# Sparse attention and a two-layer projection on one core: the first three batches run as sequences of their own, w_out is loaded ahead of batch 2, and the masking and copying of these batches is spread over three engines

## The chip, the cores and the metric

The kernel runs on one core of one Trainium2 chip. The metric is the device time of one execution in microseconds (us); lower is better. Every timed kernel was run four times, and the kernel before was run beside it on the same chip. A profile is of one execution: its span is about 2 us shorter than the time of the same run, because the span is counted from the first to the last instruction. The granted clock, or PEclk, is the share of the full TensorE clock that the profile shows as granted, 1.00 at most.

Engine names are those of the profile: PE is TensorE, DVE is VectorE, ACT is ScalarE, POOL is GpSimd, SP is SyncE; a trailing q (SPq) is the queue from which that engine issues DMAs.

## The reference

```python
def _attn_ref(q, k, v):                      # each (8, 8, 576, 64): batch, heads, tokens, width
    B, H, S, D = q.shape
    stride = 32
    scores = np.matmul(q, k.transpose(0, 1, 3, 2)) / np.sqrt(D)
    rel = pos[:, None] - pos[None, :]
    mask_local = (rel >= 0) & (rel < stride)                      # heads 0 to 3
    mask_strided = (rel >= 0) & (pos[None] % stride == pos[:, None] % stride)   # heads 4 to 7
    ...                                      # masked softmax, then attn @ v

def _moe_ref(x, w_in, w_out, alpha):         # x: the 4608 tokens of attention output, 512 wide
    h = x @ w_in                             # 512 -> 2048
    g = np.maximum(h, 0.0) + alpha * np.minimum(h, 0.0)
    return g @ w_out                         # 2048 -> 512
```

So there are eight batches of attention, each with four local and four strided heads, and then two projections over 4608 tokens, which the kernel takes in nine chunks of 512.

## The kernel before

A batch has two units, the strided one and the local one. Each unit has two pairs of heads. The attention of a unit is cut into pieces: two transposes (T, of q and of k), three scores for each pair (Sc), two or three products with v for each pair (Pv), and one transpose of the output for each pair (X). The pieces that matter here:

```python
def transpose_piece(u, nm):
    tp = pspool.tile([128, 8, 64, 2], F16, tag="ps", name="tp")     # PSUM
    ...                                                             # 8 transposes on PE
    if nm == "q":
        for hh in range(2):                                         # two halves of 64 partitions
            rr = slice(64 * hh, 64 * hh + 64)
            keep(nc.vector.tensor_copy(split(qpads[u % 2][rr, :, hh, :])[0], main[rr]))
        return
    ...
    keep(nc.scalar.copy(ko[0], main))                               # kT
    keep(nc.scalar.copy(ko[1], tail(0, 128, 64)))
    ...

def score_piece(P, i):
    ...                                                             # matmuls into sp
    keep(nc.scalar.activation(et[0:r, 0:n], sp[0:r, 0:n], AF.Exp, scale=SCALE))
    eng = nc.vector if P.b < 2 else nc.gpsimd                       # who multiplies by the mask
    ...
        keep(eng.tensor_tensor(ev, ev, m..., op=ALU.mult))

def pv_piece(P, a):
    ...                                                             # matmuls into pv, et as weights
    keep(nc.vector.reciprocal(rc[0:w, 0:nb], pvv[:, :, 64]))
    keep(nc.vector.tensor_tensor(P.x16..., pvv[:, :, 0:64], rc..., op=ALU.mult))
```

The program order is written out by hand. Batch 0 is done before the first projection. From batch 1 on, one rolling sequence mixes the pieces of neighbouring pairs, and the pieces are dealt out between the matmuls of the projections; fp32 to fp16 casts of q, k and v go to GpSimd along with them.

```python
for m in range(16):
    lin1_piece(0, m, True)
    if m == 8:
        ...                                  # casts of batch 1's local unit, loads of batch 2
        for c in range(4):
            load_w(c, True)                  # w_out, issued by GpSimd between batch 2's loads
    attn_n(0 if m < 12 else 1, end1)
...
for n in range(1, NCH):                      # the main loop; one n is one round
    ab = attn_until(n + 2) if n + 2 < B else len(pieces)
    for i in range(16):
        lin2_piece(n, i)
        attn_step(ab)
        if n + 1 < NCH:
            lin1_piece(n + 1, i)
            attn_step(ab)
    while pos["i"] < ab:
        attn_step(ab)                        # what is left over, in a block
```

The softmax here doesn't subtract the row's maximum and nothing guards it: scores larger than these inputs give would overflow.

## Time and profile before

| | kernel before |
|---|---|
| time, median of its first 4 runs | 363.94 us (362.0 to 365.44) |
| span of the profile, granted clock | 363.0 us, 0.953 |
| busy: PE, DVE, ACT, POOL | 329.7, 226.5, 177.6, 138.7 us |
| first matmul of lin1(0), lin1(1), lin2(0) | 32.2, 79.3, 97.7 us |
| first matmul of the main loop, of its second round | 119.1, 153.7 us |
| from there to the end | 209.3 us |

The chain of waits leads back from the last instruction to whatever released it, step by step. Its shares tell which engine the end of the kernel waited for. In the kernel before it is PE for four fifths, and DMA for a tenth:

```profile
PE 81%; DMA 9%; DVE 3%; ACT 2%; POOL 2%; issue 2%; SPq 1%; POOLq 0%; ACTq 0%
```

An engine can be busy for 60% of the span, as DVE is, and hold the chain for 3% of it. The stage marks in the table are read from the timeline of PE.

### The profile page before, as it was taken

Reading aid. Unit: us, or ns where it says so; the run is one execution under the profiler, and the core shown is the slowest. Engines: PE = TensorE matmul, PEld = TensorE weight load, DVE = VectorE, ACT = ScalarE, POOL = GpSimd, SP = SyncE. Lnnn points to the kernel's source line nnn. Section 1 sums busy time; section 2 is a strip of 40 time slices with the busy share of each in tenths; the row PEclk is TensorE's granted clock in tenths of the full one; section 3 lists DMA queues with packets and bytes.
Section 4 is the critical chain, followed back from the end, with each engine's and each line's share of the span. In section 5 each row is a group of like instructions: output and inputs, shape, how many; then the busy total and the mean of one; then the engine's idle time right before and its main releaser. Section 6 shows DMA issues by size and latency. Waiting matters only on the chain.

```text
span 363.0 us, 6353 instructions
## 1 busy us (share of the span) xinstructions
PE 329.7 (91%) x2449; PEld 185.8 (51%) x2449; DVE 226.5 (62%) x423; ACT 177.6 (49%) x328; POOL 138.7 (38%) x170
## 2 busy tenths in 40 slices
PE   6658974649998999999999999999999999999996
PEld 3353443424564455555557776555555444444444
DVE  5776898837864477758676767585767444444410
ACT  2532663516643556565656565656554544444421
POOL 5360473381576365546455564556151000000000
PEclk9977997559999999999999999999999999999999
DMA  7989999999936083519352820000000010010012
GB/s 210 218 134 287 199 238 196 275 206 280 232 103 203 32 232 96 175 42 246 96 175 53 242 63 32 29 32 29 31 32 29 29 60 29 29 60 29 29 61 87
DMA packets 52926, 44.08 MB, mean 121 GB/s; under 512 B 33616, under 2 KB 38112, under 8 KB 52896
## 3 DMA queue, kind: packets, MB, share of 16 engines
q1 hardware_dynamic: 47712, 37.11, 38.8%
q0 software_dynamic: 4640, 5.51, 8.2%
q10 hardware_dynamic: 544, 1.05, 1.0%
q8 instruction: 19, 0.31, 0.4%
q14 instruction: 11, 0.09, 0.1%
HBM read 38.42 MB, written 9.44 MB: 132 GB/s over the span
## 4 chain that ended last, share of the span: by engine, by line
PE 81%; DMA 9%; DVE 3%; ACT 2%; POOL 2%; issue 2%; SPq 1%; POOLq 0%; ACTq 0%
PE hps L437 34%; PE ops L482 34%; DMA sttl<-in_k_dram 6%; PE sp L251 4%; PE tp L210 3%; PE pv L280 3%; DMA stv<-in_v_dram 3%; PE xp L297 2%; SPq L100 1%; PE ops L473 1%; DVE et L266 1%; DVE x L289 1%; ACT osb L487 1%; POOL vs L151 1%; ACT et L259 0%
## 5 line engine op out<-in xcount | busy, mean ns | idle before, releaser
L437 PE MATMUL hps<-xT,win 128*128 128x512 f16 (+1 forms) x640 | 148.3, 364 | 0.8 <-DVE gT L450 0.8
L450 DVE SCALAR_TENSOR_TENSOR gT<-neg,oma,hps 128x512 f16<-128x512 f32 x144 | 106.9, 743 | 59.2 <-ACT neg L447 56.7
L482 PE MATMUL ops<-wout,gT 128*128 128x512 f16 x560 | 141.4, 379 | 2.0 <-ACT osb L487 2.0
L447 ACT ACTIVATE neg<-hps 128x512 f32<-128x512 f32 x144 | 86.2, 599 | 94.9 <-PE hps L437 94.0
L266 POOL TENSOR_TENSOR et<-et,consts 128x384 f16<-128x384 f16 (+2 forms) x60 | 54.2, 908 | 85.4 <-ACT et L259 84.5
L437 PEld LDWEIGHTS <-win 128*128 128x128 f16 x640 | 60.1, 99 | 49.8 <-issue 6.0
L482 PEld LDWEIGHTS <-gT 128*128 128x128 f16 x560 | 50.4, 98 | 49.0 <-issue 2.8
L259 ACT ACTIVATE et<-sp 128x384 f16<-128x384 f32 (+2 forms) x96 | 45.6, 490 | 24.6 <-PE sp L251 24.4
L289 DVE TENSOR_TENSOR x<-pv,rc 72x384 f16<-72x384 f32 (+2 forms) x80 | 42.2, 527 | 2.7
L223 DVE COPY qpad<-tp 64x1024 f16<-64x1024 f16 x32 | 39.0, 1220 | 3.8 <-PE tp L210 3.5
L251 PE MATMUL sp<-qpad,kT 128*128 128x144 f16 (+1 forms) x224 | 32.8, 248 | 7.2 <-DVE qpad L240 3.8
L287 DVE RECIPROCAL rc<-pv 72x6 f32<-72x6 f32 (+2 forms) x80 | 14.8, 186 | 37.5 <-PE pv L280 37.3
L280 PEld LDWEIGHTS <-et 72*128 72x128 f16 (+1 forms) x448 | 25.6, 102 | 23.7 <-POOL et L262 3.7
L251 PEld LDWEIGHTS <-kT 128*128 128x128 f16 x224 | 20.5, 103 | 25.4 <-issue 5.7
L487 ACT COPY osb<-ops 128x512 f32<-128x512 f32 x35 | 20.5, 586 | 21.9 <-PE ops L482 21.9
L236 ACT COPY kT<-tp 128x1024 f16<-128x1024 f16 x16 | 16.2, 1011 | 20.0 <-PE tp L210 20.0
L280 PE MATMUL pv<-vl,et 128*128 128x65 f16 x192 | 12.4, 201 | 8.1 <-POOL et L262 3.4
L280 PE MATMUL pv<-vs,et 72*128 72x65 f16 x256 | 16.9, 200 | 1.7 <-DVE x L289 0.9
L151 POOL CAST vs<-stv 72x1024 f16<-72x1024 f32 x16 | 16.9, 1084 | 2.9 <-DMA stv<-in_v_dram 2.9
L297 PE MATMUL xp<-consts,x 72*128 72x72 f16 (+1 forms) x224 | 15.3, 211 | 2.0 <-DVE x L289 1.7
L297 PEld LDWEIGHTS <-x 72*128 72x128 f16 (+1 forms) x224 | 12.8, 104 | 7.2 <-DVE x L289 2.4
L151 POOL CAST tl<-sttl 128x512 f16<-128x512 f32 x8 | 4.9, 618 | 28.6 <-DMA sttl<-in_k_dram 28.6
(48 smaller groups left out, 186.4 us busy)
## 6 DMA issues: line engine op xcount, KB each, us to landing
out_dram<-osb SPq DMA_DIRECT2D x35, 256.0 KB, 2.0
stq<-in_q_dram SPq DMA_DIRECT2D x16, 512.0 KB, 6.7
stk<-in_k_dram SPq DMA_DIRECT2D x12, 512.0 KB, 5.0
stv<-in_v_dram SPq DMA_DIRECT2D x7, 768.0 KB
stv<-in_v_dram SPq DMA_DIRECT2D x8, 576.0 KB
win<-in_moe_w_in_dram POOLq DMA_DIRECT2D x4, 512.0 KB, 9.3
wout<-in_moe_w_out_dram POOLq DMA_DIRECT2D x4, 512.0 KB, 13.4
stk<-in_k_dram ACTq DMA_DIRECT2D x2, 512.0 KB, 8.4
```

Source lines behind the costliest of these rows:

```text
L151: keep(nc.gpsimd.tensor_copy(o, i))
L223: keep(nc.vector.tensor_copy(split(qpads[u % 2][rr, :, hh, :])[0], main[rr]))
L251: keep(nc.tensor.matmul(sp[:, 2 * w * x : 2 * w * x + 2 * w], P.kT[:, k0 : k0 + 128], P.qpad[:, :, w * t : w * t + w], start=(x == 0), sto ...
L259: keep(nc.scalar.activation(et[0:r, 0:n], sp[0:r, 0:n], AF.Exp, scale=SCALE))
L266: keep(eng.tensor_tensor(ev, ev, m.unsqueeze(1).to_broadcast([r, n // w, w]), op=ALU.mult))
L280: keep(nc.tensor.matmul(pv[:, 65 * x : 65 * x + 65], et[0:r, c : c + 128], v16[0:r, t, 2 * P.pr + hh, :], start=(x == 0), stop=(x == nb - ...
L289: keep(nc.vector.tensor_tensor(P.x16[0:w, c0 : c0 + 64 * nb].rearrange("r (c e) -> r c e", e=64), pvv[:, :, 0:64], rc[0:w, 0:nb].unsqueeze ...
L297: keep(nc.tensor.transpose(xp[:, P.w * t : P.w * t + P.w], P.x16[0 : P.w, 128 * t : 128 * t + 128], ident[0 : P.w, 0 : P.w]))
L437: keep(nc.tensor.matmul(hps[:, dst : dst + w], win16[:, kk, 128 * m : 128 * m + 128], xT[:, kk, src : src + w], start=(kk == 0 and x == 0) ...
L447: keep(nc.scalar.activation(neg, hps, AF.Relu, scale=-1.0))
L450: keep(nc.vector.scalar_tensor_tensor(gTs[n][:, m, :], neg, oma[:, m : m + 1], hps, op0=ALU.mult, op1=ALU.add))
L482: keep(nc.tensor.matmul(ops, gTs[n][:, kf, 128 * mt : 128 * mt + 128], wout16[:, kf, :], start=(kf == 0), stop=(kf == 15)))
```

## The change

The intent is to have the first three batches ready sooner. Each of them becomes a sequence of its own, in which both of its units are in flight, and no piece of a later batch stands ahead of its last pieces. w_out goes out before batch 2's loads rather than among them. For these batches, the mask multiplies alternate between DVE and GpSimd, and one of the two copies of a transposed q goes to ScalarE. Twelve buffers hold the exponentials (et) instead of eight. The first three steps of the main loop take no attention pieces, so that GpSimd gets ahead.

```diff
-    NE = 8
+    NE = 12
...
-                keep(nc.vector.tensor_copy(split(qpads[u % 2][rr, :, hh, :])[0], main[rr]))
+                copy = nc.scalar.copy if b < 3 and hh else nc.vector.tensor_copy
+                keep(copy(split(qpads[u % 2][rr, :, hh, :])[0], main[rr]))
...
-        eng = nc.vector if P.b < 2 else nc.gpsimd
+        eng = nc.vector if P.b < 3 and i % 2 == 0 else nc.gpsimd
...
+    def first(u0, u1, order):            # one batch: transposes, scores, pv, x of both units
+        ...
+    first(1, 0, 0)
+    first(2, 3, 1)
+    first(4, 5, 1)
...                                       # the rolling sequence starts with batch 3
...                                       # batch 0: w_in's quarters go out later (steps 8 and 15)
     for m in range(16):
         lin1_piece(0, m, True)
         if m == 8:
             ...
-            load_part(2, False, "qk")
-            ...
-            for c in range(4):
-                load_w(c, True)
         attn_n(0 if m < 12 else 1, end1)
+    cast_part(1, True, "q", 0, "pool")
+    cast_part(1, True, "k", 0, "pool")
+    for c in range(4):
+        load_w(c, True)
+    keep(nc.sync.dma_start(gate[:, 16:32], wout16[:, 7, 496:512]))
+    ...                                   # batch 2's loads, batch 1's strided v casts
     while pos["i"] < end1:
         attn_step(end1)
     for m in range(16):
         lin1_piece(1, m, True)
-        attn_n(0 if m < 8 else 1, end2)
+        attn_n(0, end2)
...                                       # casts of batch 2, loads of batch 3 among lin2(0)
+    cast_tail(3, "pool")                  # ahead of the main loop: casts of batch 3, loads of 4
+    cast_part(3, False, "q", 0, "pool")
+    ...
     for n in range(1, NCH):
         for i in range(16):
+            now = 0 if n == 1 and i < 3 else ab
             lin2_piece(n, i)
-            attn_step(ab)
+            attn_step(now)
```

More of the change, by code (lines that the diff above doesn't have):

```diff
@@ L324, in X, with sc, pv, tr @@
         return lambda: x_piece(pairs[g])
-    feed(T(1, "q"), 0)
-    feed(T(1, "k"), 0)
-    for g in (2, 3):
-        for i in range(3):
-            feed(Sc(g, i), 0)
-    for g in (2, 3):
-        for i in range(3):
-            feed(Pv(g, i), 0)
-    feed(T(0, "q"), 0)
-    feed(T(0, "k"), 0)
-    feed(X(2), 0)
-    feed(X(3), 0)
-    for g in (0, 1):
-        for i in range(3):
-            feed(Sc(g, i), 0)
-    for g in (0, 1):
-        for i in range(2):
-            feed(Pv(g, i), 0)
-    feed(X(0), 0)
-    feed(X(1), 3)
+    def first(u0, u1, order):
+        A, Bp = (2 * u0, 2 * u0 + 1), (2 * u1, 2 * u1 + 1)
+        def sc(gs):
+            for g in gs:
+                for i in range(3):
+                    feed(Sc(g, i), -1)
+        def pv(gs):
+            for g in gs:
+                for i in range(len(pairs[g].pgroups)):
+                    feed(Pv(g, i), -1)
+        def tr(u):
+            feed(T(u, "q"), -1)
+            feed(T(u, "k"), -1)
+        def xs(gs, last=False):
+            for g in gs:
+                feed(X(g), g if last else -1)
+        tr(u0)
+        sc(A)
+        if order == 0:
+            tr(u1)
+            sc(Bp)
+            pv(A)
+            xs(A)
+        else:
+            pv(A)
+            tr(u1)
+            xs(A)
+            sc(Bp)
+        pv(Bp)
+        xs(Bp)
+    first(1, 0, 0)
     end0 = len(pieces)
+    first(2, 3, 1)
+    end1 = len(pieces)
+    first(4, 5, 1)
+    end2 = len(pieces)
     casts = []
@@ L354, in plan_casts @@
         u = (g + 3) // 2
-        if u >= 2 * B or u < 2:
+        if u >= 2 * B or u < 7:
             return []
@@ L359, in plan_casts @@
         return [(b, strided, nm, pr) for nm, pr in names]
-    for g in range(3, npair + 2):
+    for g in range(11, npair + 2):
         a, p, t, x = g, g - 1, g + 1, g - 2
-        okA = 4 <= a < npair
-        okP = 4 <= p < npair
-        okT = 4 <= t < npair and t % 2 == 0
-        okX = 4 <= x < npair
+        okA = 12 <= a < npair
+        okP = 12 <= p < npair
+        okT = 12 <= t < npair and t % 2 == 0
+        okX = 12 <= x < npair
         nP = len(pairs[p].pgroups) if okP else 0
@@ L530 @@
     cast_tail(0, "pool")
-    cast_part(0, True, "v", 0, "pool")
-    cast_part(0, True, "v", 1, "pool")
-    cast_part(0, False, "v", 0, "pool")
-    load_w(0, False)
-    cast_part(0, False, "v", 1, "pool")
-    load_w(1, False)
-    load_w(2, False)
-    load_w(3, False)
     apt = pspool.tile([128, 512], F32, tag="ps", name="apt")
     for i in range(end0):
-        if i == 8:
-            cast_part(0, False, "q", 0, "dve")
-            cast_part(0, False, "k", 0, "act")
-        attn_step(end0)
-        if i < 2:
-            warm(4)
-        elif i < 14:
-            warm(1)
-        if i == 13:
+        if i == 2:
             keep(nc.vector.tensor_copy(id16, ident[0:16, 0:16]))
@@ L553 @@
                 oma, apt[:, 0:16], -1.0, 1.0, op0=ALU.mult, op1=ALU.add))
-    gate = cpool.tile([128, 16], F16)
-    keep(nc.sync.dma_start(gate, win16[:, 0, 1008:1024]))
+        if i == 5:
+            cast_part(0, True, "v", 0, "pool")
+        if i == 8:
+            cast_part(0, False, "q", 0, "dve")
+            cast_part(0, False, "k", 0, "act")
+            cast_part(0, True, "v", 1, "pool")
+            load_w(0, False)
+        attn_step(end0)
+        if i == 15:
+            cast_part(0, False, "v", 0, "pool")
+            load_w(1, False)
+            cast_part(0, False, "v", 1, "pool")
+            load_w(2, False)
+            load_w(3, False)
+        if i < 2:
+            warm(4)
+        elif i < 16:
+            warm(1)
+    gate = cpool.tile([128, 32], F16)
+    keep(nc.sync.dma_start(gate[:, 0:16], win16[:, 0, 1008:1024]))
     for strided in (False, True):
@@ L567, in attn_n @@
             attn_step(0)
-    end1 = attn_until(1)
     for m in range(16):
@@ L576 @@
             cast_part(1, False, "k", 0, "pool")
-            load_part(2, False, "qk")
             for pr in range(2):
                 cast_part(1, False, "v", pr, "pool")
-            load_part(2, False, "v")
-            for c in range(4):
-                load_w(c, True)
         attn_n(0 if m < 12 else 1, end1)
+    cast_part(1, True, "q", 0, "pool")
[3 more added lines that the diff above has]
+    keep(nc.sync.dma_start(gate[:, 16:32], wout16[:, 7, 496:512]))
+    load_part(2, False, "qk")
+    load_part(2, False, "v")
+    load_part(2, True, "qk")
+    for pr in range(2):
+        cast_part(1, True, "v", pr, "pool")
+    load_part(2, True, "v")
     while pos["i"] < end1:
         attn_step(end1)
-    end2 = attn_until(2)
     for m in range(16):
         lin1_piece(1, m, True)
-        attn_n(0 if m < 8 else 1, end2)
+        attn_n(0, end2)
+    cast_tail(2, "pool")
+    cast_part(2, False, "q", 0, "pool")
+    cast_part(2, False, "k", 0, "pool")
+    for pr in range(2):
+        cast_part(2, False, "v", pr, "pool")
+    load_part(3, False, "qk")
+    load_part(3, False, "v")
     for i in range(16):
@@ L592 @@
         attn_n(2, end2)
+        if i == 2:
+            cast_part(2, True, "q", 0, "pool")
+            cast_part(2, True, "k", 0, "pool")
+            load_part(3, True, "qk")
+        if i == 5:
+            for pr in range(2):
+                cast_part(2, True, "v", pr, "pool")
+            load_part(3, True, "v")
     while pos["i"] < end2:
         attn_step(end2)
+    cast_tail(3, "pool")
+    cast_part(3, False, "q", 0, "pool")
+    cast_part(3, False, "k", 0, "pool")
+    load_part(4, False, "qk")
+    for pr in range(2):
+        cast_part(3, False, "v", pr, "pool")
+    load_part(4, False, "v")
     for n in range(1, NCH):
@@ L598 @@
         for i in range(16):
+            now = 0 if n == 1 and i < 3 else ab
             lin2_piece(n, i)
-            attn_step(ab)
+            attn_step(now)
             if n + 1 < NCH:
                 lin1_piece(n + 1, i)
-                attn_step(ab)
+                attn_step(now)
         while pos["i"] < ab:
```

## The prediction

> **What bounds the kernel now.** I read the page first, part 2 above all, then the chain of waits cut to 20 to 125 us, then the timeline and the queue of DMA issues for the same stretch. Names: a batch has a local unit (heads 0 to 3) and a strided unit (4 to 7), each of two pairs of heads. lin1(n) and lin2(n) are the two projections of the n-th 512 tokens, 64 matmuls each. The main loop starts with lin2(1).
>
> ```profile
> PE   6658974649998999999999999999999999999996
> ...
> DVE  5776898837864477758676767585767444444410
> ...
> PEclk9977997559999999999999999999999999999999
> DMA  7989999999936083519352820000000010010012
> ```
>
> One digit is 9.07 us. From slice 13 (119 us) on, PE reads 8 or 9 to the end; before that it falls to 4 and its clock to half, while DMA reads 9. So the kernel has two regimes, and the change can win only in the first. The chain of waits for 20 to 125 us shows what sets that regime (start, duration, what):
>
> ```profile
> 32.20 10.46 PE hps L437 x40
> ...
> 44.42 13.93 DMA sttl<-in_k_dram
> ...
> 59.13 1.03 POOL q L151
> 60.16 1.14 POOL k L151
> 61.31 3.18 SPq L100
> 64.59 0.61 SPq L100
> 65.29 9.59 DMA stv<-in_v_dram
> 74.94 2.04 POOL vs L151 x2
> 76.97 0.88 POOL et L266
> ...
> 79.52 9.71 PE hps L437 x36
> ```
>
> lin1(0) starts at 32.2, lin1(1) only at 79.5. In between batch 1 should finish, but its last pieces stand behind pieces of batch 2 in PE's order, and those wait for batch 2's loads and GpSimd's casts. The timelines of GpSimd and of the DMA queue show why the loads are late:
>
> ```profile
> 45.03 2.99 POOL L493 DMA_DIRECT2D wout<-in_moe_w_out_dram  x4
> ```
>
> ```profile
> 44.42 0.78 SPq L109 DMA_DIRECT2D sttl<-in_k_dram  x1
> ...
> 46.37 18.11 SPq L100 DMA_DIRECT2D stq<-in_q_dram  x1
> ```
>
> w_out goes out in the middle of batch 2's loads; the tail then takes 13.9 us, and the next load is stuck in its issue for 18 us. Other marks from the same chain: lin2(0) starts at 97.7, the main loop at 119.1, its second round at 153.9.
>
> **What the Trainium skill says.** "Perfetto Trace Analysis", section "Optimizing Scalar/DVE Operations": work of a saturated DVE may go to ScalarE or GpSimd, but GpSimd and DVE share an SBUF read port, so moving work between those two may not help. The trace agrees: a 128x384 mask multiply on DVE had a mean of 0.38 us (L266), but the one at 50.0 us, beside GpSimd casts, took 1.21. "GPSIMD Engine Reference", 4.1: about 2 times slower for two inputs. It agrees (by shape, means in ns):
>
> ```profile
> L266 POOL TENSOR_TENSOR et<-et,consts 72x432 f16<-72x432 f16 x24 | 23.9, 998 | 18.3 <-ACT et L259 17.5
> ...
> L266 DVE TENSOR_TENSOR et<-et,consts 72x432 f16<-72x432 f16 x8 | 4.2, 539 | 1.8 <-ACT et L259 1.8
> ```
>
> "DMA: Bandwidth & Descriptors", "Issuing engines are not separate DMA queues": all queues interleave on the same 16 engines. It agrees: the 13.9 us tail beside w_out, against a least of 4.9. "TensorE: Matmul & The Clock Gate", "What's actually happening": half clock after an idle window of about 3.4 us, full again after as long a busy one. It agrees: PEclk is 0.5 from 60 to 80 us, and lin1(1)'s first 38 matmuls took 9.9 us against 38 x 0.2155 = 8.2, a cost of 1.7.
>
> **Batch 0: about -0.8 us.** Before, DVE is nearly full from 16.8 to 32.6 us. The change gives ScalarE one of two qpad copies in each of two transposes (2 x 1.22 us) and GpSimd 4 of 12 multiplies (about 1.8 us), so some 4 us leave DVE. But the scores of the second unit now stand ahead of the first unit's output in DVE's order. By hand: local cast ends 16.5, qpad 18.5, the tails after ScalarE's kT 20.1, scores 20.2, six exponentials of 0.5 to 23.5, multiplies 23.9; then six reciprocal and scale steps of 0.66 (27.9), four of 0.69 (30.7), xT. lin1(0) starts at 31.4 instead of 32.2.
>
> **w_in goes out later: against the change.** GpSimd's order now puts two local multiplies and a value cast before w_in's second quarter, which went out at 20.1 and now can at about 24.7. The gate for batch 1's loads reads that quarter. Before it opened at 28.6, with the first quarter in the way; I take 31.5, and batch 1's tail at 43.5 to 44 instead of 40.95. Its transpose stood at 45.1, so most of this fits in slack; I charge 0.5 to 1 us.
>
> **Batch 1 alone: the gain.** lin1(0) ends near 50.5 with two scores done. GpSimd ends the multiply of local score 2 at 52.4. Next in its order stand the strided q and k casts (2.1), the issue of w_out (3.0) and two value casts (2.1), and only then the multiply of local score 5 (0.9): 60.5. PE is in order and the pv of that score waits for it, so this is my critical wait. After it: pv and transposes 1.2, qpad 1.2 and tails with ScalarE's 1.3 in between to 64.6, six strided exponentials and multiplies to 68.4, six output steps of 0.68 to 72.5, transposes and xT. lin1(1) starts at 73 instead of 79.5: -6.5.
>
> **lin1(1) and lin2(0): +1.6.** Before, they took 39.6 us together, with 30 attention steps among them. After, lin1(1) is bare: 64 x 0.2155 = 13.8, plus the cold 1.7, 15.5. lin2(0) carries 30 steps, two per quarter. The pitch of such a quarter before was (114.79 - 97.85) / 11 = 1.54 us; 15 of those, one bare 0.9, and 1.6 for the first score, which waits for its copies, make 25.6. Sum 41.1. Batch 2's loads should not limit this: w_out goes out at 54 to 57, its second quarter opens the gate near 63, and the local half lands near 80, against a need at 88.5.
>
> **What moves into the main loop: +5.7.** Before, 8 pieces of batch 3 were done by 119.1; now none. The order of instructions shows 26 pieces inside the first round and 12 in a block at its end. The first round was 153.9 - 119.1 = 34.8: 27.6 of projections and 30 pieces, so 0.24 each. After: 27.6 + 26 x 0.24 = 33.8. The block: the score waits for kT 1.2, its multiply ends at 3.1, two value casts of 1.05 on GpSimd, one multiply to 6.1, pv and two transposes to 7.0. Sum 40.8 less 34.8 is 6.0; I take 5.7 because the first three steps let GpSimd get ahead.
>
> **Sum.** -6.5 (with batch 0 and the late w_in inside it) + 1.6 + 5.7 = +0.8, so 363.8 us: the gain of the first regime is mostly spent again. The rest is the same instructions at PE's pace.
>
> **Rivals.**
> A: GpSimd doesn't hold the local pv (w_out's issue and casts overlap better), batch 1 ends at 67, and the block at the end of the first round costs 3. Then -12.5 + 1 + 3 = -8.5: 354.5. For it: batch 0, the same work, took from 13 to 32.6 us with everything on DVE, 19.6 us where I gave 24. Against it: the order of GpSimd's instructions.
> B: DMA becomes the bound. The gated chain (batch 1, then w_out, then batch 2) lets DMA idle from about 48 to 56. If the gate of w_out opens at 68 and batch 2 lands at 90, lin2(0) waits 5 us: 369. For it: small packets made batch 2's tail take 13.9 us. Against it: 7 us of slack by my count.
> C: the shared port slows DVE's multiplies and GpSimd's together in the dense stretches, by 0.5 us for each of some 16 on the path, of which perhaps a third shows: +3.
> D: the first half gains as in A, and the block is nearly free since PE only shifts work: 351.
>
> **Range and chances.** My sum says 363.8; I think my hand chains count stalls too fully (rival A measured 19.6 where I take 24), and weigh A and D at 35% together, B and C at 15%. 0.5 x 363.8 + 0.35 x 353 + 0.15 x 367.5 is 360.6; I say 360.5, with 352 to 368 for 8 in 10. Faster by 2% means under 355.8, which most of A and D reach: 0.24. Slower by 2% means over 370.3: 0.05.
>
> **What would show it.** Right: lin1(0) near 31.4; GpSimd's multiply of local score 5 right after the strided value casts near 60, with PE's pv waiting for it; lin1(1) near 73; lin2(0) of 25 us; main loop near 114; a gap of 4 us on PE at the end of the first round near 150; from the second round on the same pace as before. Wrong: lin1(1) before 69 or after 76, a DMA wait ahead of batch 2's casts while PE stands, or no gap at the end of the first round.

## The result, and the profile after

The changed kernel took 387.5 us, median of 4 runs (386.58 to 388.3), against 363.94 us (362.0 to 365.44) of the kernel before. The ratio is 1.065, with a 95% interval of 1.0587 to 1.0712. Here and below, a ratio is the mean time of one kernel's fast runs over the mean of the other's fast runs of the same rounds, so it is not quite the ratio of the medians. Executions over 1.5% slower than the fastest of the same kernel are left out of the means. The outputs were correct. The change made the kernel 6.5% slower. The prediction gave most weight to a result within 2%, and its range of 352 to 368 does not hold the result.

The marks show where the time went (us, from the timelines of PE; each is the first matmul of that stage):

| | lin1(0) | lin1(1) | lin2(0) | main loop | 2nd round | end |
|---|---|---|---|---|---|---|
| before | 32.2 | 79.3 | 97.7 | 119.1 | 153.7 | 363.0 |
| predicted in the hand sum | 31.4 | 73 | 88.5 | 114 | 154.6 | 363.8 |
| after | 34.4 | 77.7 | 93.4 | 131.3 | 175.6 | 385.4 |

From the second round to the end both kernels take the same: 209.3 and 209.8 us. The loss of 22.4 us lies before it: 12.2 by the start of the main loop (131.3 - 119.1), 9.7 in the first round (44.3 against 34.6), 0.5 in the rest. It isn't more work: DVE is busy for 229.5 us against 226.5, ACT for 183.5 against 177.6, POOL for 140.7 against 138.7. The slices of the page (one digit is 9.63 us now) show the dips:

```profile
PE   6568963599775899979999999999999999999996
...
DVE  5556874758448367686777676768666544444410
...
PEclk9986995679889599998999999999999999999999
DMA  7849938999320299854836182000001001101012
```

The dip at 58 to 77 us is still there (5 and 6 in PEclk), and new ones stand at 97 to 135 us: PE reads 7, 7, 5, the clock 8, 8, and then 5 in the slice from 125 us. DMA reads 3, 2, 0, 2 there, so this is no wait for a transfer. The shares of the chain after say who it is:

```profile
PE 71%; DMA 9%; DVE 8%; ACT 5%; POOL 4%; issue 2%; SPq 1%; ACTq 0%; POOLq 0%
```

PE's share fell by 10 points, and DVE, ACT and POOL rose from 7 to 17 together: these are the engines over which the vector work was spread. The chain from 116 to 129 us (start, duration, what) names one instruction:

```profile
117.73 6.95 DVE et L267
...
128.89 1.72 PE ops L504 x4
```

L267 is a mask multiply, the last strided one of batch 2, on 72 partitions by 288 columns. The five others of its shape on DVE took 3.5 us together (six took 10.5). It took 6.95 us. GpSimd's timeline for that stretch (start, duration, engine, line, operation):

```profile
117.48 1.00 POOL L267 TENSOR_TENSOR et<-et,consts 72x432 f16<-72x432 f16 x1 [2.35 <-ACT et L260]
118.43 0.61 POOL L151 CAST tl<-sttl 128x512 f16<-128x512 f32 x1
...
123.49 1.04 POOL L151 CAST k<-stk 128x1024 f16<-128x1024 f32 x1
```

GpSimd has no gap from 117.48 to 124.53. DVE's multiply was issued 0.25 us after GpSimd's first instruction of that run, and ended at 124.68, with GpSimd's last. PE meanwhile waited for what follows that multiply:

```profile
125.43 0.30 PE L281 MATMUL pv<-vs,et 72*128 72x65 f16 x4 [4.60 <-DVE x L290]
```

The number in brackets is idle time of PE just before, and who ended it. After these 4.6 us, four matmuls took 1.72 us in the chain instead of 0.86 (its second line above). In the timeline the groups of four took 1.65 to 1.91 us until 136 us, instead of 1.03, and the mean clock from 125 to 136 us was 0.54.

The prediction had named another wait, in batch 1. It is there: on GpSimd the multiply of local score 5 stands behind two casts, the issue of w_out and two value casts, and PE waits for it.

```profile
55.65 1.16 POOL L151 CAST q<-stq 128x1024 f16<-128x1024 f32 x1
...
57.87 3.03 POOL L515 DMA_DIRECT2D wout<-in_moe_w_out_dram  x4
60.86 2.08 POOL L151 CAST vs<-stv 72x1024 f16<-72x1024 f32 x2
62.86 0.94 POOL L267 TENSOR_TENSOR et<-et,consts 128x384 f16<-128x384 f16 x1
```

```profile
63.86 0.62 PE L281 MATMUL pv<-vl,et 128*128 128x65 f16 x8 [6.49 <-POOL et L267]
```

A third thing is in the view of waits (who waited for whom: us in total, times, longest). It has a line that the kernel before has not:

```profile
ACT qpad L224 <- DVE qpad L224: 25.0, 6, 10.6
```

ScalarE's half of the copy of a transposed q waits for DVE's half, in all six transposes of the first three batches: each time it starts within 0.04 us of the end of DVE's half. The 25.0 us are ScalarE's idle time up to there, and part of it is time in which ScalarE had no work anyway. The split was to run the two halves side by side.

### The profile page after: what moved, and what is told of

The parts are those of the page before. It is cut to its first block, busy times and chain, and to the rows that moved or that the text cites. A ratio compares the mean times of both kernels' runs of the same rounds, so it can differ in the third digit from the quotient of the medians.

```text
span 385.4 us, 6354 instructions
## 1 busy us (share of the span) xinstructions
PE 339.9 (88%) x2451; PEld 188.3 (49%) x2451; DVE 229.5 (60%) x417; ACT 183.5 (48%) x334; POOL 140.7 (37%) x174
## 4 chain that ended last, share of the span: by engine, by line
PE 71%; DMA 9%; DVE 8%; ACT 5%; POOL 4%; issue 2%; SPq 1%; ACTq 0%; POOLq 0%
PE ops L504 30%; PE hps L459 29%; DMA stv<-in_v_dram 6%; PE sp L252 4%; DVE et L267 3%; PE tp L210 3%; DVE x L290 2%; PE pv L281 2%; DMA consts<-consts 2%; ACT kT L237 2%; PE xp L298 2%; DVE qpad L224 2%; DMA win<-in_moe_w_in_dram 1%; ACT qpad L224 1%; ACT et L260 1%
## 5 line engine op out<-in xcount | busy, mean ns | idle before, releaser
L504 PE MATMUL ops<-wout,gT 128*128 128x512 f16 x560 | 148.1, 391 | 3.8 <-ACT osb L509 3.8
L267 POOL TENSOR_TENSOR et<-et,consts 72x432 f16<-72x432 f16 (+2 forms) x62 | 57.8, 936 | 105.2 <-ACT et L260 104.4
L504 PEld LDWEIGHTS <-gT 128*128 128x128 f16 x560 | 52.1, 100 | 53.6 <-issue 9.7
L260 ACT ACTIVATE et<-sp 128x384 f16<-128x384 f32 (+2 forms) x96 | 44.3, 490 | 19.8 <-PE sp L252 19.8
L252 PE MATMUL sp<-qpad,kT 128*128 128x144 f16 (+1 forms) x224 | 31.2, 245 | 9.3 <-ACT kT L237 6.0
L281 PEld LDWEIGHTS <-et 72*128 72x128 f16 (+1 forms) x448 | 24.1, 104 | 28.0 <-POOL et L267 10.4
L224 DVE COPY qpad<-tp 64x1024 f16<-64x1024 f16 x26 | 31.7, 1217 | 4.1 <-PE tp L210 3.9
L267 DVE TENSOR_TENSOR et<-et,consts 72x432 f16<-72x432 f16 (+2 forms) x18 | 18.2, 1030 | 10.2 <-ACT et L260 10.2
L298 PE MATMUL xp<-consts,x 72*128 72x72 f16 (+1 forms) x224 | 17.4, 219 | 5.2 <-DVE x L290 5.0
L302 ACT COPY xT<-xp 128x576 f16<-128x576 f16 x16 | 10.2, 636 | 23.6 <-PE xp L298 23.6
L241 DVE COPY qpad<-tt 64x128 f16<-64x128 f16 x32 | 8.2, 255 | 21.4 <-ACT kT L238 21.0
```

Of the source, the lines that this page charges most:

```text
L224: keep(copy(split(qpads[u % 2][rr, :, hh, :])[0], main[rr]))
L252: keep(nc.tensor.matmul(sp[:, 2 * w * x : 2 * w * x + 2 * w], P.kT[:, k0 : k0 + 128], P.qpad[:, :, w * t : w * t + w], start=(x == 0), sto ...
L267: keep(eng.tensor_tensor(ev, ev, m.unsqueeze(1).to_broadcast([r, n // w, w]), op=ALU.mult))
L281: keep(nc.tensor.matmul(pv[:, 65 * x : 65 * x + 65], et[0:r, c : c + 128], v16[0:r, t, 2 * P.pr + hh, :], start=(x == 0), stop=(x == nb - ...
L298: keep(nc.tensor.transpose(xp[:, P.w * t : P.w * t + P.w], P.x16[0 : P.w, 128 * t : 128 * t + 128], ident[0 : P.w, 0 : P.w]))
L504: keep(nc.tensor.matmul(ops, gTs[n][:, kf, 128 * mt : 128 * mt + 128], wout16[:, kf, :], start=(kf == 0), stop=(kf == 15)))
```

## Experiments

The theory (A in the expectations, in its several parts) was: the spread of vector work costs the time, through (1) one DVE multiply held up by GpSimd's run of casts, (2) the copy split that doesn't run in parallel, (3) the wait for GpSimd in batch 1, and (4) the block of pieces at the end of the first round; the new order itself is good. The rivals were that the late issue of w_in or the order of w_out sets the marks, that the multiply of (1) is only a symptom of a wait that would show elsewhere, and that the order of pieces is itself at fault. Each run undoes or adds one part. All edits are against the changed kernel unless said otherwise, and all outputs were correct. The changed kernel was not run again with them; the kernel before was, and its median differed by at most 1.1 us (363.48 to 364.54), so differences of medians from 387.5 are good to about 1 us.

### Moving one multiply

```diff
-        eng = nc.vector if P.b < 3 and i % 2 == 0 else nc.gpsimd
+        eng = nc.vector if P.b < 3 and i % 2 == 0 and (P.g, i) != (11, 2) else nc.gpsimd
```

> One of the 96 mask multiplies, the last one of batch 2 (72x288, local name: pair 11, third score), moves from DVE to GpSimd. In the changed kernel it took 6.95 us on DVE while GpSimd ran six casts back to back. Theory A (GpSimd's stream holds the SBUF ports that this multiply needs, and DVE gets them only at a gap): that wait goes, the six output steps behind it start near 118.5 instead of 124.6, PE isn't idle for 4.6 us and its clock doesn't fall, so lin2(0) ends 6 to 8 us earlier and the total is 378 to 381 us, 1.6 to 2.3% faster than the changed kernel. Rival B (the long record is only where DVE shows a wait for something else, such as the exponential or a buffer): DVE stays stuck at the same place and the total stays at 386 to 388.

It took 378.0 us (377.21 to 378.54), ratio 1.0377 [1.0333, 1.0422]. One multiply of 96 was given to GpSimd, where it stands ahead of the casts, and the kernel became 9.5 us faster. The main loop starts at 123.9 instead of 131.3 (-7.4), and its first round takes 42.0 us instead of 44.3 (-2.3). The second part is the clock: PE did not stand idle, and its clock stays at 1.00 from 110 to 134 us.

### Holding the casts back instead

The multiply stays on DVE, and GpSimd gets a copy of one element that needs the multiply's result. This makes a gap in GpSimd's run without moving any work.

```diff
+    held = cpool.tile([1, 1], F16)
...                                          # at the end of score_piece
+        if (P.g, i) == (11, 2):
+            keep(nc.gpsimd.tensor_copy(held, et[0:1, 0:1]))
```

> No multiply changes its engine. One 1x1 copy on GpSimd, which reads the result of the last multiply of batch 2, is put ahead of the burst of casts for batch 3, so the burst can't start before DVE has done that multiply; all else as changed. Theory A (DVE can't get the SBUF ports while GpSimd's instructions follow each other without a gap): the multiply takes 0.3 to 1.3 us instead of 6.95, the output steps start 5 to 6 us earlier, and the total is 377 to 381, as when the multiply itself was moved (378.0). Rival B (moving the multiply helped because DVE had one instruction fewer, or because of something else that this record hides): the total stays at 386 to 388, or gets worse by the wait that is added to GpSimd.

It took 378.99 us (378.42 to 379.38), ratio 1.0424 [1.0396, 1.0452], 8.5 us less than the changed kernel. The timelines of DVE and of GpSimd:

```profile
117.24 0.91 DVE L268 TENSOR_TENSOR et<-et,consts 72x288 f16<-72x288 f16 x1 [1.42 <-ACT et L261]
```

```profile
116.99 1.00 POOL L268 TENSOR_TENSOR et<-et,consts 72x432 f16<-72x432 f16 x1 [2.73 <-ACT et L261]
118.21 0.18 POOL L271 COPY held<-et 1x1 f16<-1x1 f16 x1 [0.23 <-DVE et L268]
118.34 0.60 POOL L152 CAST tl<-sttl 128x512 f16<-128x512 f32 x1
```

The same multiply now takes 0.91 us: it ends (118.15) just after the one GpSimd multiply beside it (117.99). So neither the instruction nor its data was slow; it was held by the GpSimd instructions that followed. That DVE gets in only at a gap, as the theory has it, does not hold in general. Other DVE multiplies of the changed kernel also started while GpSimd instructions followed each other without a gap. Six of them ended about 0.2 us after the one instruction that was then running (the one at 55.83 us ended at 57.02, the q cast at 56.81, and the k cast behind it ran on to 57.92); one did not wait at all, and one that began 0.05 us before the end of a cast waited for the next cast too. What makes this one wait for the whole run is not shown. The Trainium skill, "SBUF — State Buffer", section "Who interferes with whom", says that a DVE instruction with two inputs in SBUF contends with a GpSimd instruction that reads SBUF, and that whichever issues second "fully blocks until the first finishes" (its summary has these words). The trace agrees with the blocking and with its length in those six; here it differs: the wait didn't end with the first GpSimd instruction but with a run of eight, a multiply and seven casts, 6.95 us later.

### All multiplies of batches 0 and 1 back on DVE, all of batch 2 on GpSimd

```diff
-        eng = nc.vector if P.b < 3 and i % 2 == 0 else nc.gpsimd
+        eng = nc.vector if P.b < 2 else nc.gpsimd
```

> The mask multiplies go back to the engines they had before: DVE alone for batches 0 and 1, GpSimd alone for batch 2; all else as changed. Theory A (shared ports): batch 2 gains as in the run that moves one multiply, 7 to 9 us, and Pv of the local unit of batch 1 no longer waits 6.5 us for GpSimd's multiply behind its casts, so lin1(1) starts 3 to 6 us earlier and w_in goes out 3 us earlier as well; total 372 to 376. Rival C (spreading really relieves DVE, and only the one collision is bad): batches 0 and 1 get slower by the 8 multiplies of 0.4 us that come back, and the total is 380 to 383.

It took 373.71 us (372.49 to 375.17), ratio 1.0263 [1.0211, 1.0315], 13.8 us less than the changed kernel and the largest single part. lin1(1) starts at 71.5 instead of 77.7, because the local multiply no longer stands behind the casts; the main loop starts at 117.4 instead of 131.3. In both kernels 24 multiplies run on DVE, but in the changed one they take 21.5 us and here 11.9. Sorted by whether GpSimd was working at the time: in the changed kernel 14 overlap GpSimd's work and have a mean of 1.28 us (0.84 without the one of 6.95), 10 do not and have a mean of 0.36; in the kernel before 9 overlap, with a mean of 0.74, and 15 do not, with a mean of 0.35.

### The same spread in the kernel before

This edit is against the kernel before, and takes the spread of the multiplies alone.

```diff
-        eng = nc.vector if P.b < 2 else nc.gpsimd
+        eng = nc.vector if P.b < 3 and i % 2 == 0 else nc.gpsimd
```

> The kernel before with the change's split of mask multiplies alone (two of three on DVE, one on GpSimd, in batches 0 to 2). The same 24 multiplies' worth of work lies on DVE as before. Theory A (the split puts multiplies behind GpSimd's casts, and DVE's beside them): DVE's multiplies take 14 to 22 us in sum instead of 11.9 and the total gets worse by 4 to 15 us, 367 to 378. Rival C (the split is only bad in the changed order): within 1% of before, 360 to 367.

It took 366.69 us, ratio 1.0092 [1.0042, 1.0142]. My theory had it slower by more, and DVE's 24 multiplies at 14 to 22 us in sum; they took 13.6. The rival, within 1%, fits better, though the interval reaches 1.4%. lin1(0) starts 6.8 us later (39.0 against 32.2): PE waits 7.33 us for a multiply that GpSimd does behind its casts and the issue of w_in. But lin1(1) starts at 79.7 against 79.3: the wait for batch 2's loads, which the change removes, swallowed it. And no multiply met as long a run of casts: the longest took 2.03 us, through two casts that followed each other without a gap. So the spread is not costly everywhere. It is costly in the new order, where one multiply meets a run of seven casts, and where no later wait hides it.

### Both halves of the copy on DVE again

```diff
-                copy = nc.scalar.copy if b < 3 and hh else nc.vector.tensor_copy
+                copy = nc.vector.tensor_copy
```

> Both halves of the qpad copy go back to DVE in all six transposes; all else as changed. Theory A: ScalarE's half is made to wait for DVE's half (25.0 us of waiting, 6 times), so the split saves DVE 1.2 us but puts ScalarE's 1.0 ahead of its kT copy; without it kT starts at once and the scores come about 1 us earlier per unit, 4 to 6 us in all: 381 to 384. Rival D: DVE is what paces these stretches, so 6 x 1.22 us more on DVE cost 3 to 7 us: 390 to 394.

It took 380.98 us (380.85 to 381.15), ratio 1.0463 [1.0412, 1.0513], 6.5 us less than the changed kernel. For one transpose, the timeline of the changed kernel:

```profile
94.88 1.22 DVE L224 COPY qpad<-tp 64x1024 f16<-64x1024 f16 x1
96.13 1.01 ACT L224 COPY qpad<-tp 64x1024 f16<-64x1024 f16 x1 [1.96 <-DVE qpad L224]
97.17 1.01 ACT L237 COPY kT<-tp 128x1024 f16<-128x1024 f16 x1
98.23 0.58 PE L252 MATMUL sp<-qpad,kT 128*128 128x192 f16 x4 [1.97 <-ACT kT L237]
```

and of this run:

```profile
93.34 2.46 DVE L224 COPY qpad<-tp 64x1024 f16<-64x1024 f16 x2
93.78 1.01 ACT L237 COPY kT<-tp 128x1024 f16<-128x1024 f16 x1 [1.16 <-PE tp L210]
95.85 0.49 PE L252 MATMUL sp<-qpad,kT 128*128 128x192 f16 x4 [1.13 <-DVE qpad L224]
```

In the first, three copies stand one behind another, 1.22 + 1.01 + 1.01, because ScalarE's half waits for DVE's, and kT comes after it on ScalarE. In the second, kT runs beside the two halves on DVE. From the start of the transposes of q to the first score it is 4.0 us in the first (98.23 - 94.23) and 3.2 in the second (95.85 - 92.69), and PE stood idle for the last 1.97 and 1.13 of it. The view of stretches shows what this does to the clock (columns: stretch, its length, busy us and count of PE, PEld, DVE, ACT, POOL, then the clock, DMA's share, GB/s). The changed kernel, and this run in the same stage:

```profile
98.00:103.00 5.00, 4.57 (x20) 2.43 (x21) 2.31 (x5) 2.58 (x8) 2.87 (x3) 0.66 0.02 7
...
109.00:116.00 7.00, 4.53 (x23) 2.52 (x21) 1.93 (x6) 3.94 (x8) 1.00 (x1) 0.76 0.11 40
```

```profile
95.00:99.00 4.00, 2.88 (x20) 1.78 (x20) 2.65 (x6) 2.31 (x6) 1.84 (x2) 1.00 0.48 174
...
105.00:109.00 4.00, 3.61 (x26) 1.94 (x26) 3.10 (x8) 1.99 (x5) 1.00 (x1) 1.00 0.19 70
```

After both transposes of batch 2 the clock fell to 0.66 and 0.76 in the changed kernel; here it stays at 1.00. By the marks, 6.0 of the 6.5 us are gained between the start of lin2(0) and the main loop (31.9 us instead of 37.9). The starved multiply is still there, and still takes 6.95 us: this part is separate from it.

### Both halves on ScalarE, kT on DVE

```diff
-                copy = nc.scalar.copy if b < 3 and hh else nc.vector.tensor_copy
+                copy = nc.scalar.copy if b < 3 else nc.vector.tensor_copy
...
-        keep(nc.scalar.copy(ko[0], main))
+        keep((nc.vector.tensor_copy if b < 3 else nc.scalar.copy)(ko[0], main))
```

> For batches 0 to 2 ScalarE takes both halves of the qpad copy and DVE the kT copy, so the two engines read two different PSUM tiles instead of one; all else as changed. Theory A (what cost time was the wait of one engine for the other at the one tile, not the spreading itself): ScalarE 2.0 us and DVE 1.2 us run beside each other and the total falls at least as much as with both halves on DVE (381.0): 379 to 382. Rival H (ScalarE is too busy with exponentials and evictions to take more): 383 to 388.

It took 378.89 us (378.55 to 379.97), ratio 1.043 [1.0392, 1.0468], 8.6 us less than the changed kernel and 2.1 less than the run with both halves on DVE. Its timeline of the same transpose:

```profile
90.84 2.02 ACT L224 COPY qpad<-tp 64x1024 f16<-64x1024 f16 x2 [0.71 <-PE tp L210]
91.29 1.23 DVE L237 COPY kT<-tp 128x1024 f16<-128x1024 f16 x1 [0.38 <-PE tp L210]
```

The two engines now work on different PSUM tiles, and neither waits for the other; the first score follows 2.7 us after the start of the transposes (92.92 - 90.20). ScalarE also does a half in 1.01 us where DVE takes 1.22. So relieving DVE by way of ScalarE was a sound idea; what spoilt it was the cut through one tile, where one half waits for the other. The Trainium skill, "PSUM — Partial Sum Buffer", section "PSUM bank collisions raise a hardware error", says that two engines must not touch the same bank and quadrant of 32 partitions at once, that different quadrants are safe, and that guarding by bank is the simple version. The halves here lie in partitions 0 to 63 and 64 to 127, so by the page they could overlap; the program as built makes ScalarE wait for DVE all the same. No run here tried the overlap.

### w_out's issue after batch 1

The rest of batch 1's pieces is put ahead of the strided casts and of w_out.

```diff
+    attn_n(4, end1)
     cast_part(1, True, "q", 0, "pool")
```

> Four attention steps (the scores of batch 1's local unit) are emitted ahead of the strided casts and the issue of w_out, so GpSimd does the multiply of local score 5 before them instead of after. Theory A (PE stands 6.5 us at the pv that waits for it): the wait goes, but the strided q cast and w_out come 1 us later; lin1(1) starts at 72 to 75 instead of 77.9. As lin2(0) needs batch 2, whose loads wait for w_out and would be about 1 us later, with slack of some 10 us, the total falls by 3 to 5: 382.5 to 384.5. Rival E (the strided casts or batch 2's loads are what limits): unchanged within 1 us.

It took 380.89 us (379.81 to 383.19), ratio 1.0467 [1.041, 1.0523], 6.6 us less than the changed kernel, more than I had expected. PE's pv no longer waits 6.49 us for GpSimd, but 0.55 and 0.47, and lin1(1) starts at 72.3 instead of 77.7 (-5.4). None of this is given back: the main loop starts 6.7 us earlier. Moving the multiplies back to DVE removes the same wait, so I don't expect the two gains to add; no run makes both edits.

### w_in early again

```diff
         if i == 8:
             ...
-            load_w(0, False)
+            for c in range(4):
+                load_w(c, False)
...                                          # and no load_w(1..3) at step 15
```

> All four quarters of w_in go out together at the place where the changed kernel sends the first, ahead of GpSimd's two local multiplies; all else as changed. In the changed kernel the second quarter went out at 27.0 us and the gate for batch 1's loads opened at 32.5. Theory A (that delay reaches the path: batch 1's tail lands at 46.3 and PE waits 0.8 us for the q cast, and the strided and value casts shift too): gate near 29, tail near 42, lin1(1) 1.5 to 4 us earlier than 77.7, total 382 to 385.5. Rival F (the delay is hidden behind lin1(0), as I predicted in part): lin1(1) within 1 us, total 386 to 388.

It took 387.69 us (387.18 to 388.54), ratio 1.0662 [1.0619, 1.0706]: the same as the changed kernel. I had expected a gain; the rival, that this is hidden, is right. The gate for batch 1's loads (a small DMA that reads part of w_in, so that the loads queued behind it wait for w_in) did open earlier, at 29.98 us instead of 32.48, and the cast of batch 1's tail ran at 42.02 instead of 46.34. But PE came to the transpose of batch 1 only at 49.40, against 47.99 in the changed kernel, since lin1(0) began 1.9 us later (36.2). The data waited for PE. In the changed kernel PE had waited 0.82 us for the q cast at that transpose, so no more than that was to be gained there. The edit is not free either: it puts four issues, 3.08 us, instead of one, 0.84 us, ahead of GpSimd's two local multiplies, which start at 24.95 and 27.16 instead of 23.63 and 25.27.

### No pause in the first three steps of the main loop

```diff
-            now = 0 if n == 1 and i < 3 else ab
+            now = ab
```

> The first three steps of the main loop carry attention pieces too, so 32 pieces of batch 3 lie inside the first round and 6 in the block at its end, instead of 26 and 12; all else as changed. Theory A (the block costs PE time because its pieces wait on each other): the first round, 44.3 us in the changed kernel, becomes 2 to 4 us shorter, total 383.5 to 385.5. Rival G (the block ends with a wait for the strided values of batch 4, whose load stands in the DMA queue behind an output that is issued near the end of the round, whatever is in the block): the round stays within 1 us, total 386.5 to 388.

It took 380.6 us (379.19 to 381.69), ratio 1.047 [1.0424, 1.0515], 6.9 us less than the changed kernel, where I had expected 2 to 4. The first round takes 40.2 us instead of 44.3. In the changed kernel its projections end at 168.4, and the second round starts at 175.6, so the block of leftover pieces takes 7.2 us. PE is idle for 3.0 of them, 1.83 in a wait for GpSimd:

```profile
174.17 0.29 PE L281 MATMUL pv<-vl,et 128*128 128x65 f16 x2 [1.83 <-POOL et L267]
...
175.60 1.73 PE L504 MATMUL ops<-wout,gT 128*128 128x512 f16 x4
```

The last line is slow as well, 1.73 us for four matmuls instead of the 1.03 that this view shows elsewhere; the clock's mean from 165 to 176 us was 0.89. Of the gain, 4.1 us lie in the round and 0.7 in an earlier start; a further 0.7 lies after it, and 1.4 only in the timed runs and not in the profiles (379.9 against 385.4, 5.5 us).

### The new order with the four parts undone

Multiplies as in the kernel before, both halves of the copy on DVE, w_in early, no pause. These four are edits, and not the four parts of the theory above: the first of them undoes (1) and (3), the second (2), the last (4).

> Four repairs together: mask multiplies on the engines of before, both halves of the qpad copy on DVE, w_in sent together, attention in all steps of the main loop; what is left of the change is the order of the pieces (each batch on its own) and w_out ahead of batch 2. Taken one by one the first two gave 13.8 and 6.5 us against the changed kernel; of the 6.5 perhaps half is left once DVE carries all multiplies of batches 0 and 1, and I give 2 us each to the other two. From 373.7: 365 to 368, so within 1.5% of before. If the order of the pieces is itself worth what I predicted (main loop 5 us earlier), it is at 362; if the order costs, it stays above 369.

It took 360.91 us (359.07 to 364.23), ratio 0.994 [0.9867, 1.0013]. The single gains were 6.5 + 13.8 + 6.9 - 0.2 = 27.0, and together they gave 387.5 - 360.9 = 26.6, so nothing large is missing. The time is below the 365 to 368 that I expected. That the sum fits within 0.4 us is closer than this run can tell, as its four times lie between 359.07 and 364.23. What is left is the order of pieces, w_out's place and the twelve buffers. They bring the main loop forward to 113.6 us, 5.6 before that of the kernel before, and lose 3.7 of it in the first round (38.3 against 34.6). No run takes these three apart.

### The same with the copies on different tiles

The four parts as in the last run, but the copies as in the run with both halves on ScalarE and kT on DVE.

> As the four repairs together, but ScalarE takes both halves of the qpad copy and DVE the kT copy in batches 0 to 2 (that was 2 us better than both on DVE, with the rest as changed). If the 2 us add: 358 to 360. If DVE, which has all multiplies of batches 0 and 1 here, gains more from giving away 2.4 us per unit and taking 1.2: 354 to 358. If ScalarE becomes what the scores wait for: 361 to 364.

It took 358.33 us (357.82 to 358.75), ratio 0.9856 [0.983, 0.9883]. The main loop starts at 109.3.

### And with the leftover pieces spread

Six more pieces are dealt out in the last steps of the first round.

```diff
                 lin1_piece(n + 1, i)
                 attn_step(now)
+                if n == 1 and i >= 10:
+                    attn_step(now)
```

> As the run above, with one more attention piece in each of the last six steps of the first round of the main loop, so that no block of attention pieces is left at its end. If the block costs by its pieces' waiting on each other, as the first round of the four repairs suggests (38.2 us against 34.5 before, with 8 pieces or 1.9 us more in it), the round becomes 1 to 2 us shorter. If the pieces then wait inside the round instead (GpSimd's multiplies and casts pace them), no difference within 1 us.

It took 357.07 us (356.58 to 358.28), ratio 0.9833 [0.9797, 0.9869], the fastest of all versions here and 1.7% faster than the kernel before. The first round takes 37.3 us instead of 38.3. The step from the last version is 1.3 us, and the two intervals overlap, so it is likely rather than certain. The slices of its page, 8.87 us each:

```profile
PE   5867986898798999999999999999999999999996
...
PEclk9696998699899999999999999999999999999999
```

The deep dips at 97 to 135 us are gone (one 7 is left, in slice 10 of the first row), and PE reads 8 or 9 from slice 12 (106 us) on, as it did in the kernel before from 119.

The marks of all runs (us, one profile each; the last column is the longest mask multiply on DVE):

| run | lin1(0) | lin1(1) | lin2(0) | main loop | 2nd round | span | longest |
|---|---|---|---|---|---|---|---|
| before | 32.2 | 79.3 | 97.7 | 119.1 | 153.7 | 363.0 | 1.21 |
| after | 34.4 | 77.7 | 93.4 | 131.3 | 175.6 | 385.4 | 6.95 |
| one multiply moved | 35.6 | 78.8 | 95.3 | 123.9 | 165.9 | 376.8 | 1.21 |
| casts held back | 34.2 | 76.8 | 92.9 | 123.9 | 165.8 | 377.0 | 1.21 |
| multiplies as before | 33.2 | 71.5 | 87.2 | 117.4 | 159.3 | 370.7 | 1.22 |
| both halves on DVE | 34.1 | 75.9 | 91.8 | 123.7 | 167.8 | 379.1 | 6.95 |
| halves on ScalarE, kT on DVE | 32.5 | 73.1 | 89.3 | 121.2 | 165.4 | 376.8 | 6.95 |
| w_out later | 34.1 | 72.3 | 88.5 | 124.6 | 168.4 | 379.6 | 6.94 |
| w_in early | 36.2 | 79.3 | 95.6 | 131.6 | 175.5 | 386.7 | 6.95 |
| no pause | 35.0 | 78.3 | 94.8 | 130.7 | 170.8 | 379.9 | 6.95 |
| spread in the kernel before | 39.0 | 79.7 | 98.0 | 120.1 | 154.7 | 363.9 | 2.03 |
| four parts undone | 33.3 | 68.4 | 85.0 | 113.6 | 151.8 | 360.9 | 1.13 |
| the same, copies on two tiles | 32.1 | 65.5 | 80.8 | 109.3 | 147.6 | 356.7 | 1.14 |
| and leftovers spread | 32.1 | 64.1 | 80.4 | 108.4 | 145.7 | 354.8 | 0.81 |

The marks up to lin1(0) move by about 2 us between kernels that ought to be alike there (34.1 to 35.6 in the changed kernel and in the runs that touch only later stages), so shifts of that size in a single profile are not read as effects.

## Why the prediction was wrong

The hand sum was 363.8 us; the profile's span is 385.4. The difference of 21.6 us falls on four of its terms: 4.7 up to lin1(1) (77.7 against 73), 12.5 from there to the main loop (53.6 against 41.1), 3.8 in the first round (44.3 against 40.5) and 0.6 in the rest.

- **"lin1(1) and lin2(0): +1.6" is the step that failed.** lin1(1) itself was right: 15.7 us measured, 15.5 predicted. lin2(0) took 37.9 us where I had 25.6. I took the pitch of a quarter from the kernel before, 1.54 us, where all of a unit's multiplies were on one engine. In the new order PE stood 4.6 us for the one starved multiply, and the clock that fell with it slowed what came after; moving that multiply, or holding the casts back, gave 9.5 and 8.5 us, and undoing the split copy took 6.0 us out of this stage. About 3 of the 12.3 us are of another kind, since lin2(0) takes 28.6 us with the multiply moved and 28.5 with the four parts undone: there the pitch itself was too small. The sum also has two slips. From 97.85 to 114.79 the chain of the kernel before has twelve quarters and not eleven, which makes the pitch 1.41 us and lin2(0) 23.7; and the 38 matmuls of the cold start are 36 (x36 in the line shown), which makes its cost 2.0 us and not 1.7. Without them the sum would have been 39.5 and not 41.1, still further from the 53.6 measured. Rival C, "the shared port slows DVE's multiplies and GpSimd's together", had the engines right, and I sized it as 0.5 us for each of 16, "of which perhaps a third shows: +3". The slowing was not spread evenly: the 24 multiplies took 9.6 us more (21.5 - 11.9), some 6.6 of it in one instruction (6.95 us, against 0.30 for its shape beside no GpSimd work), at a place where PE had nothing else to do.
- **The copies were assumed to run side by side.** In "Batch 0: about -0.8", I took two copies of 1.22 us off DVE and put "qpad 18.5", as if ScalarE worked beside it, and in batch 1 again "qpad 1.2 and tails with ScalarE's 1.3 in between". They ran one after the other, with kT behind them. Undoing the split gave 6.5 us and doing it on two tiles 8.6. Only 0.3 of the 6.5 us came by lin1(0) and 1.8 by lin1(1), so these two terms were off by little; the rest came in lin2(0), where "1.6 for the first score, which waits for its copies" was the term, and the clock fell after the wait. I had read the diff for who does the work, and not the order of instructions for who waits for whom; the order with its waits might have shown it before any run.
- **"Batch 1 alone: the gain" was right in kind.** The multiply of local score 5 stood right after the value casts, and PE waited for it, as predicted, with 6.49 us. It ended at 63.8 us instead of 60.5, since GpSimd's run began later than I had it (46.34 instead of 43.5 to 44 for the tail, and 2.46 us of waiting for v). From there to lin1(1) it took 13.9 us where I had 12.5. The gain by lin1(1) was 1.6 us instead of 6.5, and 77.7 lies beyond the 76 that I had named as a sign of being wrong. Rival A, that GpSimd doesn't hold the local pv, was wrong.
- **"w_in goes out later: against the change"** charged little (0.5 to 1 us), and nothing speaks against that: sending w_in early gave no gain, though that run had a cost of its own.
- **"What moves into the main loop: +5.7"** was right for the block, 7.2 us measured against 7.0, and 3.8 short for the round. The clock is what was left out: the first matmuls of the round came after the standstill, and took 1.7 to 1.9 us for four instead of 1.03 up to 136 us. Without the starved multiply the round took 42.0, within 1.5 of the prediction.
- **"The rest is the same instructions at PE's pace"** was right: 209.8 against 209.3 us. So was that DMA wouldn't be the bound (rival B); that small packets made the 13.9 us tail, as it says there, no run tests.
- **The order of pieces**, with w_out's place and the twelve buffers, gains without the spread: with the four parts undone the main loop starts 5.6 us earlier than in the kernel before. I had 5 for the whole change, and that this is so near is luck: lin1(1) starts 4.6 us before my 73, since no multiply of batch 1 is on GpSimd in that run, and lin1(1) and lin2(0) take 4.1 us more than my 41.1. The fastest version has a span of 354.8 us, beside my 363.8 and rival A's 354.5, though not for rival A's reason.

The chances failed with it: I had put slower by more than 2% at 0.05. The weight went to the question whether my chains counted stalls too fully; they counted too few. What stays open is why one multiply was held through eight GpSimd instructions when others got in after one, why ScalarE's half is made to wait, and whether the halves could safely overlap; no run tried it. It is also open how much of the 1.4 us that the run without the pause gained in its timed runs beyond its profile is noise.

## What to carry to other kernels

Before moving two-input elementwise work onto DVE or GpSimd, look at what the other of the two does at that moment, not at its mean busy share: here one multiply of 96, beside a run of casts without a gap, cost 8.5 to 9.5 us, and either a gap or another engine for it removed that. Six others that met such runs lost less than 0.9 us each, so look for the one that PE waits for. Split work between engines along tiles rather than through one tile, and check in the order of instructions that neither half waits for the other. Where the first engine in line has nothing else to do, count the wait and also the clock after it.

## What the Trainium skill lacked or had wrong

- "SBUF — State Buffer", "Who interferes with whom" and the summary: it says that the second to issue blocks until the first finishes. Here a DVE multiply stayed blocked through a run of eight GpSimd instructions without a gap, 6.95 us, and took 0.91 us once the seven casts were held back behind it. Six others of the same kernel that met such runs did get in after the first instruction. The page has no word of when a run of instructions keeps the other out.
- "Perfetto Trace Analysis", "Optimizing Scalar/DVE Operations": that moving work between DVE and GpSimd might not help is right, but the section gives no size. Here the same number of DVE multiplies, 24, took 21.5 us instead of 11.9, and those beside GpSimd's work had a mean of 1.28 us (0.84 without the longest) against 0.36 for those clear of it.
- "PSUM — Partial Sum Buffer", "PSUM bank collisions raise a hardware error": it doesn't say what a guard on the whole tile costs where quadrants would do. Here the copies of one tile's two halves by ScalarE and DVE ran one after the other in all six cases, and copying two tiles at once by the same engines made the kernel 8.6 us faster. That such a guard is what made ScalarE wait is not shown.
